# Attention's output products as column tiles: two of 64 for the values, four of 32 for the feature sums

## The chip, the cores and the metric

One core of a Trainium2 chip runs the whole program. The metric is the device time in microseconds of one execution; the figure for a kernel is the median of its runs. The engines are TensorE (PE, with its weight loads listed apart as PEld), VectorE (DVE), ScalarE (ACT), GpSimd (POOL) and SyncE (SP), whose queue issues the transfers.

## What is computed

The reference is a linear attention with exponential features, then two multilayer products:

```python
def phi(x):
    proj = np.einsum('bhsd,df->bhsf', x, w_phi)            # 4 x 8 heads, 576 rows, 64 -> 128
    proj = proj - np.max(np.abs(proj), axis=-1, keepdims=True)
    return np.concatenate([np.exp(proj), np.exp(-proj)], axis=-1)
q_p, k_p = phi(q), phi(k)
kv  = np.einsum('bhsf,bhsd->bhfd', k_p, v)
z   = np.sum(k_p, axis=2)
num = np.einsum('bhsf,bhfd->bhsd', q_p, kv)
den = np.einsum('bhsf,bhf->bhs', q_p, z)[..., None] + 1e-06
x   = (num / den)                                           # heads side by side: 2304 x 512
x   = ((x @ w1) * (x @ w2)) @ w3 @ w_out                    # 512 -> 1024 -> 1024 -> 512
x   = np.maximum(x @ w_in, 0) ** 2 @ w2_out                 # 512 -> 2048 -> 512
```

The weights come as float64 and are decoded on the chip.

## The kernel before

**Attention** goes over 16 pairs of heads (4 batches x 4 pairs), one pair a slot. The order of every instruction in a slot is written by hand in the list SLOT (L36): each name is a step, taken for the pair of the slot or, by an offset in the table `steps` (L575), for the pair before or after. So slot t projects the queries and keys of pair t, prepares those of pair t + 1, and makes the output of pair t - 1. All five engines run strictly in that order (manual schedule, L649).

The steps around the change: `project_q` and `project_k0`, `project_k1` are the feature projections. `max_q` (L386), `max_rows` (a transposition on PE, L394) and `max_parts` (L396) make the maxima of the query rows, which go through a transfer to `mrow` and are subtracted on PE in `minus_q`. `keep_values` (L445) copies kv of a pair to SBUF for the products: for each sign and head a 128 x 128 stationary tile whose 128 columns are the 64 values and the feature sum z repeated 64 times. `out00` to `out11` (L452) multiply it with the features of one head and one half (288) of the rows, for both signs; 64 of the output's partitions are the numerators and the other 64 all hold the denominator. `keep00` to `keep11` (L460) copy the banks to SBUF, `denominators` (L465) take one copy of the denominators out by a transposing reduction, `reciprocals` (L475) invert and spread them, `quotients` (L484) multiply on POOL, `store_x` (L498) writes x for two pairs to HBM.

PSUM in attention is a pool "t" of three banks, a pool "o" of two for the products, and three banks of projected queries.

**Weights** are decoded beside all this. One tile of 128 x 512 takes a transfer to one of four `raw` places (L99), one ACT step, four on DVE (L108 to L118) and one on POOL (L123); those that are split into a high and a low part take one more on ACT and POOL. The list `beside` (L542) is decoded in attention by the steps w-1, w0 and w1 of the slots, one tile after another; the list `need` (L528) is fetched by `prefetch` and decoded after it, `many` (L811) tiles in a step (one unless the table says otherwise), as `begin` (L692) finds room among LEFT and RIGHT places.

**After attention** the w3 tiles are transposed and multiplied with w_out (`Fold`, L767), a fold a step in the first eight steps, while the products with w1 and w2 and the folded weight run over five blocks of rows, twice. Then the last two products run over the same blocks (L958).

Of the kernel before, what the change touches and what calls it, by code (L numbers as in the profile page):

```python
# [18 lines left out]
C = 4  # L19
TAIL = 64  # L20
LEFT = 20
RIGHT = 13

# [8 lines left out]
tail_values/0  # L34
""".split()
SLOT = """  # L36
load_kq product_b project_k0 keep_values turn_w3b split_w3b x_load project_q project_k1 less_max_k0 max_q turn_k out00 max_rows x_split0 max_parts w-1 store_x less_max_k1 x_split2 out01 exp_k0 x_split1 keep00 w1 high_k out10 keep01 turn_q0 out11 w1 keep_q0 project_k2 denominators0 keep10 w0 keep11 low_k less_max_k2 values0 gate turn_w3 exp_k1 denominators1 x_split3 exp_k2 w0 w0 w0 turn_q1 reciprocals keep_q1 minus_q product_a0 exp_q0 values1 exp_q1 turn_tails keep_tails split_q split_w3 low_tail low_q product_a1 quotients keep_a load_v tail_values
""".split()


# [1 line left out]
def attention_then_mlps(ctx: ExitStack, tc: tile.TileContext, q, k, v, w_phi, w1, w2, w3, wo, wi2, wo2, out):  # L42
# [31 lines left out]
    def temps(name):  # L74

        turn[0] += 1
        y_of, t_of = pools[turn[0] % 2 % len(pools)], 0
        if len(pools) > 1:
            t_of = 0 if room_t[0] else 1
            assert room_t[t_of], name  # L80
            room_t[t_of] -= 1
            home_t[name] = t_of
        y = y_of.tile([P, 512], I32, tag="dy", bufs=2, name=f"dy_{name}")
        t = pools[t_of].tile([P, 512], I32, tag="dt", bufs=2 if t_of else 3, name=f"dt_{name}")
        return y, t

    def done_t(name):
        room_t[home_t.pop(name, 0)] += 1

    turn, room_t, home_t = [0], [3, 2], {}  # L90


    def decoding(src, name, got):
# [42 lines left out]
    def finish(steps):  # L136
        for _ in steps:
            pass
# [59 lines left out]
    with ExitStack() as actx:  # L198
# [3 lines left out]
        def bank(name, tag="t", bufs=3):  # L202
            return ps.tile([P, 512], F32, tag=tag, bufs=bufs, name=name)
# [186 lines left out]

        def max_rows(z):

            z["pm"] = bank(f"pm_{z['nm']}")[:, 0:P]
            nc.tensor.transpose(z["pm"], z["m1"], ident)  # L394

        def max_parts(z):  # L396
            pm = z["pm"][0:2 * nb]
            m = att.tile([2 * nb, 32], F32, tag="m", name=f"m_{z['nm']}")
            nc.vector.tensor_reduce(m, pm.rearrange("p (a r) -> p r a", a=4), AX.X, ALU.max)
            mh = att.tile([2 * nb, 2, 32], F32R, tag="mh", name=f"mh_{z['nm']}")  # L400
            nc.vector.tensor_copy(mh[:, 0], m)
            nc.vector.tensor_tensor(out=mh[:, 1], in0=m, in1=mh[:, 0].bitcast(F32), op=ALU.subtract)
            z["mrow"] = mrow
            for s in range(2):
                nc.sync.dma_start(
                    z["mrow"][s:s + 1].bitcast(F32).rearrange("s (k r) -> s k r", r=32), mh[:, s].bitcast(F32)
                )
# [36 lines left out]

        def keep_values(z):  # L445

            z["kv"] = att.tile([P, 2, 2, P], F32, tag="kv", name=f"kv_{z['nm']}")
            kv = z["kv"].rearrange("p s j (h d) -> p s (j h) d", d=D)
            nc.scalar.copy(kv[:, :, 0::3, :], z["pkv"][:, :, :, 0:D])
            nc.scalar.copy(kv[:, :, 1:3, :], z["pkv"][:, :, :, D:].to_broadcast([P, 2, 2, D]))  # L450

        def out_half(z, j, s):  # L452
            z["po", j, s] = po = bank(f"po_{z['nm']}_{j}_{s}", "o", 2)
            for e in range(2):
                nc.tensor.matmul(  # L455
                    po[:, 0:HALF], z["kv"][:, e, j, :], z["qp"][:, e, j, s * HALF:(s + 1) * HALF],
                    start=e == 0, stop=e == 1,
                )

        def keep_half(z, j, s):  # L460
            if j + s == 0:
                z["nd"] = att.tile([P, 2, S], F32, tag="nd", name=f"nd_{z['nm']}")
            nc.scalar.copy(z["nd"][:, j, s * HALF:(s + 1) * HALF], z["po", j, s][:, 0:HALF])

        def denominators(z, j):  # L465

            if j == 0:
                z["dc"] = att.tile([P, nb], F32, tag="dc", name=f"dc_{z['nm']}")
            nc.vector.tensor_reduce(
                z["dc"][j * D:(j + 1) * D],  # L470
                z["nd"][(1 - j) * D:(2 - j) * D, j].rearrange("p (n r) -> p n r", r=32),
                AX.X, ALU.max, apply_transpose=True,
            )

        def reciprocals(z):  # L475
            rc = att.tile([P, nb], F32, tag="rc", name=f"rc_{z['nm']}")
            nc.vector.tensor_scalar(out=rc, in0=z["dc"], scalar1=1e-6, scalar2=None, op0=ALU.add)
            nc.vector.reciprocal(rc, rc)
            z["rb"] = att.tile([P, S], F32, tag="rb", bufs=1, name=f"rb_{z['nm']}")
            nc.vector.transpose(  # L480
                z["rb"].rearrange("p (n r) -> p n r", r=32), rc.unsqueeze(2).to_broadcast([P, nb, 32])
            )

        def quotients(z):  # L484
            b, pr = z["b"], z["pr"]
            if pr % 2 == 0:
                xm[b] = unit(F32, [2, C * P], f"xm_{b}_{pr // 2}")
            for j in range(2):
                h = slice(j * D, (j + 1) * D)
                nc.gpsimd.tensor_tensor(  # L490
                    out=xm[b][h, pr % 2, :], in0=z["nd"][h, j, 0:C * P], in1=z["rb"][h, 0:C * P], op=ALU.mult
                )
                nc.gpsimd.tensor_tensor(
                    out=xt[h, pr, b * TAIL:(b + 1) * TAIL], in0=z["nd"][h, j, C * P:], in1=z["rb"][h, C * P:],
                    op=ALU.mult,
                )

        def store_x(z):  # L498
            b, pr = z["b"], z["pr"]
# [5 lines left out]
        def w3_of(i):  # L505
            kc, g = divmod(i, 2)
            return w3[kc * P:(kc + 1) * P, g * 512:(g + 1) * 512], f"w3_{i}"
# [17 lines left out]
                return got, decode_splitting(src, name, w12, lambda *a: take(*a)), 1  # L525
            return got, decode_splitting(w2_of(i), f"w2_{i}", got, lambda *a: take(*a)), 1

        need = [("w3", 2), ("w3", 3), ("w12", 6), ("w3", 4), ("w3", 5), ("w12", 7)]  # L528
        need += [("w3", i) for i in range(6, 2 * NG)] + [("w12", i) for i in range(8, 2 * NG)]
        need += [("w2", i) for i in range(2 * NR)]  # L530
        reserve, owed, room_raw = [5], [0], [4]
# [1 line left out]
        def prefetch(n=4):  # L533
            while need and room_raw[0] and len(loaded) < n:
                room_raw[0] -= 1
                kind, i = need.pop(0)
                got, steps, places = plan(kind, i)
                next(steps)
                loaded.append((kind, i, got, steps, places))
# [1 line left out]

        beside = [decode_splitting(rows(wo, j), f"wo{j}", wos) for j in range(NG)]  # L542
        beside += [decode_splitting(*w12_of(i), w12) for i in range(6)]
        beside += [decoding(*w3_of(i), w3s) for i in range(2)]
        beside.append(iter(()))
        load_kq(0)
        minus = att.tile([P, P], F32R, bufs=1, name="minus")
        nc.vector.memset(minus.bitcast(F32), -1.0)
# [22 lines left out]
        def even(f, *at):  # L571
# [7 lines left out]
            "turn_k": (1, turn_k), "high_k": (1, high_k), "low_k": (1, low_k),  # L579
            "split_q": (2, split_q), "low_q": (2, low_q), "low_q0": (2, lambda z: low_q(z, nc.vector)),  # L580
            "turn_tails": (1, turn_tails), "keep_tails": (1, keep_tails), "low_tail": (1, low_tail),
            "tail_values": (0, tail_values), "reciprocals": (-1, reciprocals), "quotients": (-1, quotients), "store_x": (-2, store_x),
            "load_kq": (2, lambda z: load_kq(live.index(z))), "load_v": (2, load_v),
        }
        for j in range(2):
            steps[f"turn_q{j}"] = 1, lambda z, j=j: turn_q(z, j)
            steps[f"keep_q{j}"] = 1, lambda z, j=j: keep_q(z, j)
            steps[f"values{j}"] = 0, lambda z, j=j: values(z, j)
            steps[f"denominators{j}"] = -1, lambda z, j=j: denominators(z, j)
            for s in range(2):  # L590
                steps[f"out{j}{s}"] = -1, lambda z, j=j, s=s: out_half(z, j, s)
                steps[f"keep{j}{s}"] = -1, lambda z, j=j, s=s: keep_half(z, j, s)
        for j in range(3):
            steps[f"project_k{j}"] = 0, (even if j == 2 else lambda f, j: lambda z: f(z, j))(project_k, j)
            steps[f"less_max_k{j}"] = 0, (even if j == 2 else lambda f, j: lambda z: f(z, j))(less_max_k, j)
# [53 lines left out]
        with tc.manual_schedule(engines=mine):  # L649
            for entry in START:  # L650
                name, t = entry.split("/")
                step(name, int(t))
            for t in range(len(todo) + 2):
                for name in SLOT:
                    if f"{name}/{t}" not in START:
                        step(name, t)
                if t >= len(todo) - 1:
                    prefetch(t - len(todo) + 3)
        finish(beside[-1])


    late = ctx.enter_context(tc.tile_pool(name="late", bufs=2, side="right", reuse_waits="tile"))
# [29 lines left out]
    def begin(n):  # L692

        fresh, room = [], free["u"] + free["w"] - reserve[0] - owed[0]
        while loaded and len(fresh) < n and loaded[0][4] <= room:
            room -= loaded[0][4]
            owed[0] += loaded[0][4]
            fresh.append(loaded.pop(0))
        return fresh
# [108 lines left out]
    HG = NG // 2  # L808
    steps = [(grp, at, k) for grp in range(2) for at in range(len(order)) for k in range(HG)]
    folds = {i: i for i in range(NG)}  # L810
    many = {10: 0, 11: 0, 30: 0, 31: 0, 40: 0, 0: 3, 1: 3, 2: 2, 3: 2, 4: 2, 5: 2, 6: 2, 37: 2, 38: 2, 39: 2}  # L811
    mlp2 = mains + [tail]

    def evict_first(b, n, yp):
# [223 lines left out]
```

## Time and profile before

| | us |
|---|---|
| median of 3 runs | 983.41 |
| lowest, highest | 981.69, 985.55 |
| the profiled execution | 982.8 |
| its span on the core | 981.0 |

The profile is of one execution. Busy time counts instructions; a matmul's end is modelled, so that neighbours overlap in the list, and the pace of a run of matmuls is read from their starts or from the chain of waits. An idle engine is put down to whoever released it last.

### The profile page before, as it was taken

What the parts mean: (1) busy time and instruction counts of PE and PEld (TensorE: products, weight loads), DVE (VectorE), ACT (ScalarE), POOL (GpSimd) and SP (SyncE); (2) the same over time, 40 slices, a digit from 0 to 9 for tenths busy, and PEclk for the clock granted to TensorE, in tenths of its full rate; (3) what the DMA queues carried; (4) which work ended last, traced back from release to release, by engine and by line L of the source; (5) the groups of instructions that cost most, each with busy time, mean ns of one, the idle gap of its engine ahead of it and who ended that gap; (6) DMA issues with size and microseconds to landing.
All of it is one profiled execution on the core that took longest, in us unless ns stands there. A gap on an engine that the chain in (4) does not pass through costs nothing.

```text
span 981.0 us, 13030 instructions
## 1 busy us (share of the span) xinstructions
PE 961.5 (98%) x4944; PEld 813.3 (83%) x4944; DVE 571.6 (58%) x910; ACT 409.6 (42%) x785; POOL 252.6 (26%) x238
## 2 busy tenths in 40 slices
PE   7999999998999999999999999999999999999997
PEld 6999999986888898888888878888888888888896
DVE  6899999879756456657766488742224222322332
ACT  6888888863422343333333334432223222322322
POOL 3455555534221223333423145510000000000000
PEclk9999999999999999999999999999999999999999
DMA  6344444425232142452444432202001000100010
GB/s 177 107 132 138 130 143 133 147 87 173 85 129 65 66 163 94 150 194 81 134 165 162 165 131 87 86 1 86 0 1 55 32 1 1 64 1 1 8 37 22
DMA packets 68560, 89.11 MB, mean 91 GB/s; under 512 B 27985, under 2 KB 53137, under 8 KB 68497
## 3 DMA queue, kind: packets, MB, share of 16 engines
q1 hardware_dynamic: 68496, 88.28, 28.1%
q8 instruction: 39, 0.64, 0.3%
q14 instruction: 25, 0.20, 0.1%
HBM read 69.76 MB, written 18.35 MB: 90 GB/s over the span
## 4 chain that ended last, share of the span: by engine, by line
PE 93%; DVE 4%; issue 1%; POOL 0%; DMA 0%; ACT 0%; DVEq 0%; POOLq 0%
PE op L858 21%; PE ph L177 20%; PE pa L177 10%; PE pb L177 10%; PE yp L840 9%; PE po L455 6%; PE pkv L431 5%; PE pf L797 4%; PE pk L238 2%; PE pq L379 2%; PE pqt L310 1%; DVE dt_w L111 1%; PE pq L412 1%; PE pw L171 1%; PE pkt L293 1%
## 5 line engine op out<-in xcount | busy, mean ns | idle before, releaser
L858 PE MATMUL op<-w_w,r 128*128 128x512 f32 x864 | 215.1, 396 | 2.3 <-DVE yp L826 2.2
L858 PEld LDWEIGHTS op<-w_w,r 128*128 128x128 f32 x864 | 162.1, 189 | 39.7 <-ACT w_w L131 2.6
L982 DVE SCALAR_TENSOR_TENSOR r<-ph,t 128x512 f32<-128x512 f32 (+1 forms) x80 | 51.0, 638 | 200.4 <-ACT t L980 200.4
L177 PE MATMUL ph<-y,w_w 128*128 128x512 f32 (+1 forms) x768 | 166.0, 365 | 0.0
L177 PEld LDWEIGHTS ph<-y,w_w 128*128 128x128 f32 x768 | 133.3, 188 | 26.1
L980 ACT ACTIVATE t<-ph 128x512 f32<-128x512 f32 (+1 forms) x80 | 44.4, 555 | 223.9 <-PE ph L177 223.9
L840 PE MATMUL yp<-g,w3o 128*128 128x512 f32 (+1 forms) x480 | 108.4, 375 | 0.0
L840 PEld LDWEIGHTS yp<-g,w3o 128*128 128x128 f32 x480 | 84.5, 190 | 16.3
L123 POOL TENSOR_TENSOR dt_w<-dt_w,dy_w 128x512 f32<-128x512 f32 x48 | 63.0, 1312 | 130.9 <-DVE dy_w L118 117.6
L177 PE MATMUL pa<-c,w_w12a 128*128 128x512 f32 (+1 forms) x432 | 95.3, 369 | 0.0
L177 PE MATMUL pb<-c,w_w12b 128*128 128x512 f32 (+1 forms) x432 | 93.9, 366 | 0.0
L177 PEld LDWEIGHTS pa<-c,w_w12a 128*128 128x128 f32 x432 | 75.0, 188 | 15.3 <-ACT c L142 0.4
L177 PEld LDWEIGHTS pb<-c,w_w12b 128*128 128x128 f32 x432 | 75.2, 189 | 13.4
L990 DVE TENSOR_TENSOR r<-r,r 128x512 fp32r<-128x512 f32 (+1 forms) x80 | 51.0, 637 | 42.6 <-ACT r L988 37.9
L919 DVE TENSOR_TENSOR g<-pb,a 128x512 f32<-128x512 f32 (+1 forms) x39 | 24.8, 635 | 84.0 <-PE pb L177 83.8
L988 ACT ACTIVATE r<-r 128x512 fp32r<-128x512 f32 (+1 forms) x80 | 47.2, 590 | 59.6 <-DVE r L982 59.6
L133 POOL TENSOR_TENSOR w_w<-dt_w,w_w 128x512 fp32r<-128x512 f32 x32 | 48.5, 1517 | 90.7 <-ACT w_w L131 90.7
L455 PE MATMUL po<-qp,kv 128*128 128x288 f32 x256 | 68.8, 406 | 0.0
L431 PEld LDWEIGHTS pkv<-vs,kp 128*128 128x128 f32 x512 | 61.3, 192 | 1.0 <-DVE kp L362 0.2
L921 ACT ACTIVATE g<-g 128x512 fp32r<-128x512 f32 (+1 forms) x39 | 23.0, 589 | 91.3 <-DVE g L919 91.3
L431 PE MATMUL pkv<-vs,kp 128*128 128x65 f32 x512 | 60.6, 271 | 0.0
L911 ACT COPY a<-pa 128x512 f32<-128x512 f32 (+1 forms) x39 | 21.2, 543 | 81.3 <-PE pa L177 81.3
(132 smaller groups left out, 1405.7 us busy)
## 6 DMA issues: line engine op xcount, KB each, us to landing
x<-x_hbm SPq DMA_DIRECT2D x16, 512.0 KB
raw_w<-in_moe_w_dram SPq DMA_DIRECT2D x16, 512.0 KB
raw_w<-in_moe_w_in_dram SPq DMA_DIRECT2D x16, 512.0 KB
raw_w<-in_moe_w_out_dram SPq DMA_DIRECT2D x16, 512.0 KB
qm<-in_q_dram SPq DMA_DIRECT2D x16, 256.0 KB
km<-in_k_dram SPq DMA_DIRECT2D x16, 256.0 KB
vs<-in_v_dram SPq DMA_DIRECT2D x32, 128.0 KB
raw_wo<-in_moe_w_out_dram SPq DMA_DIRECT2D x8, 512.0 KB
```

The lines of the kernel that those rows point to most:

```text
L123: nc.gpsimd.tensor_tensor(out=w, in0=t.bitcast(F32), in1=e.bitcast(F32), op=ALU.add)
L133: nc.gpsimd.tensor_tensor(out=dst[:, 1], in0=w[0], in1=dst[:, 0].bitcast(F32), op=ALU.subtract)
L177: nc.tensor.matmul(ps[:, 0:n], a, c, start=kk + i == 0, stop=kk == KD - 1 and i == 2)
L431: nc.tensor.matmul(z["pkv"][:, s, j], z["kp", j][:, c, s, :], z["vs"][:, j, c, :], start=j + s + c == 0, stop=False, skip_group_check=True,)
L455: nc.tensor.matmul(po[:, 0:HALF], z["kv"][:, e, j, :], z["qp"][:, e, j, s * HALF:(s + 1) * HALF], start=e == 0, stop=e == 1,)
L797: nc.tensor.matmul(pf, a, c, start=g + j + n == 0, stop=g == 1 and j == 3 and n == 2)
L840: nc.tensor.matmul(blk.yp[i][:, 0:blk.n], a, d, start=c % HG + s == 0, stop=c % HG == HG - 1 and s == 2)
L858: nc.tensor.matmul(ops[i], a, d, start=j + s == 0, stop=j == NR - 1 and s == 2)
L980: nc.scalar.activation(t[:, 0:n], ph[:, 0:n], AF.Relu)
L982: nc.vector.scalar_tensor_tensor(out=r32[:, 0:n], in0=ph[:, 0:n], scalar=0.0, in1=t[:, 0:n], op0=ALU.max, op1=ALU.mult)
L988: nc.scalar.activation(r[:, 0, 0:n], r32[:, 0:n], AF.Copy)
L990: nc.vector.tensor_tensor(out=r[:, 1, 0:n], in0=r32[:, 0:n], in1=r[:, 0, 0:n].bitcast(F32), op=ALU.subtract)
```

## The change

For each pair the stationary tiles of 128 columns are replaced by tiles of 64 columns (values) and of 32 columns (the feature sum, repeated 32 times). The value products of the two heads write partitions 0 to 63 and 64 to 127 of one bank; one bank for each half of the rows. The four feature sums (two heads, two halves) write four groups of 32 partitions of one more bank, which DVE reads directly. The reciprocals, nine columns wide, are copied to the partitions of their heads by eight small POOL copies (`spread`). The quotients then need two instructions on full partitions instead of four.

With it come a new order of the slot, the transposed maxima in pool "o", a second reduction in `max_parts` instead of a cast, two more w3 tiles in the list `beside` and two fewer in `need`, a prefetch count lower by one in the last slots, one weight place less (RIGHT), two more temporary tiles (dt) on that side, a bound on the tiles begun by the free temporaries, and one tile decoded instead of two in step 39.

```diff
-RIGHT = 13
+RIGHT = 12
 SLOT = """
-load_kq product_b project_k0 keep_values turn_w3b split_w3b x_load project_q project_k1 less_max_k0 max_q turn_k out00 max_rows x_split0 max_parts w-1 store_x less_max_k1 x_split2 out01 exp_k0 x_split1 keep00 w1 high_k out10 keep01 turn_q0 out11 w1 keep_q0 project_k2 denominators0 keep10 w0 keep11 low_k less_max_k2 values0 gate turn_w3 exp_k1 denominators1 x_split3 exp_k2 w0 w0 w0 turn_q1 reciprocals keep_q1 minus_q product_a0 exp_q0 values1 exp_q1 turn_tails keep_tails split_q split_w3 low_tail low_q product_a1 quotients keep_a load_v tail_values
+load_kq product_b project_q keep_values project_k0 turn_w3b split_w3b x_load max_q project_k1 turn_k less_max_k0
+max_rows x_split0 max_parts w-1 store_x high_k out0 less_max_k1 x_split2 exp_k0 out1 x_split1 keep0 feature_sums w1
+keep1 turn_q0 w1 low_k keep_q0 project_k2 w0 less_max_k2 values0 gate turn_w3 exp_k1 denominators x_split3 exp_k2
+spread w0 w0 w0 turn_q1 keep_q1 turn_tails keep_tails minus_q product_a0 exp_q0 reciprocals values1 exp_q1 split_q
+split_w3 low_tail low_q product_a1 quotients keep_a load_v tail_values
 """.split()
...
-        t = pools[t_of].tile([P, 512], I32, tag="dt", bufs=2 if t_of else 3, name=f"dt_{name}")
+        t = pools[t_of].tile([P, 512], I32, tag="dt", bufs=4 if t_of else 3, name=f"dt_{name}")
...
-    turn, room_t, home_t = [0], [3, 2], {}
+    turn, room_t, home_t = [0], [1, 4], {}
...
-            z["pm"] = bank(f"pm_{z['nm']}")[:, 0:P]
+            z["pm"] = bank(f"pm_{z['nm']}", "o", 2)[:, 0:P]
...
-            nc.vector.tensor_copy(mh[:, 0], m)
+            nc.vector.tensor_reduce(mh[:, 0], pm.rearrange("p (a r) -> p r a", a=4), AX.X, ALU.max)
...
+            z["kv"] = att.tile([P, 2, 2, D], F32, tag="kv", name=f"kv_{z['nm']}")
+            nc.scalar.copy(z["kv"], z["pkv"][:, :, :, 0:D])
+            z["zs"] = att.tile([P, 2, 2, 32], F32, tag="zs", name=f"zs_{z['nm']}")
+            nc.scalar.copy(z["zs"], z["pkv"][:, :, :, D:].to_broadcast([P, 2, 2, 32]))
+
+        def out_half(z, s):
+            z["po", s] = po = bank(f"po_{z['nm']}_{s}", "o", 2)
             for e in range(2):
+                for j in range(2):
+                    nc.tensor.matmul(
+                        po[j * D:(j + 1) * D, 0:HALF], z["kv"][:, e, j, :],
+                        z["qp"][:, e, j, s * HALF:(s + 1) * HALF], start=e == 0, stop=e == 1,
+                    )
+
+        def feature_sums(z):
+            z["pd"] = pd = bank(f"pd_{z['nm']}", "o", 2)
+            for e in range(2):
+                for i in range(4):
+                    j, s = divmod(i, 2)
+                    nc.tensor.matmul(
+                        pd[i * 32:(i + 1) * 32, 0:HALF], z["zs"][:, e, j, :],
+                        z["qp"][:, e, j, s * HALF:(s + 1) * HALF], start=e == 0, stop=e == 1,
+                    )
+
+        def keep_half(z, s):
+            nc.scalar.copy(z["nd"][:, s * HALF:(s + 1) * HALF], z["po", s][:, 0:HALF])
+
+        def denominators(z):
+            dc = att.tile([P, nb // 2], F32, tag="dc", name=f"dc_{z['nm']}")
             nc.vector.tensor_reduce(
+                dc, z["pd"][:, 0:HALF].rearrange("p (n r) -> p n r", r=32), AX.X, ALU.max, apply_transpose=True
+            )
+            nc.vector.tensor_scalar(out=dc, in0=dc, scalar1=1e-6, scalar2=None, op0=ALU.add)
+            z["rc"] = att.tile([P, nb // 2], F32, tag="rc", name=f"rc_{z['nm']}")
+            nc.vector.reciprocal(z["rc"], dc)
+
+        def spread(z):
+            z["rc2"] = att.tile([P, 2, nb // 2], F32, tag="rc2", name=f"rc2_{z['nm']}")
+            for i in range(4):
+                for s in range(2):
+                    at = 2 * (i // 2) + s
+                    nc.gpsimd.tensor_copy(
+                        z["rc2"][i * 32:(i + 1) * 32, s, :], z["rc"][at * 32:(at + 1) * 32, :]
+                    )
...
-            for j in range(2):
-                h = slice(j * D, (j + 1) * D)
+            nc.gpsimd.tensor_tensor(
+                out=xm[b][:, pr % 2, :], in0=z["nd"][:, 0:C * P], in1=z["rb"][:, 0:C * P], op=ALU.mult
+            )
+            nc.gpsimd.tensor_tensor(
+                out=xt[:, pr, b * TAIL:(b + 1) * TAIL], in0=z["nd"][:, C * P:], in1=z["rb"][:, C * P:], op=ALU.mult
+            )
...
-        need = [("w3", 2), ("w3", 3), ("w12", 6), ("w3", 4), ("w3", 5), ("w12", 7)]
+        need = [("w12", 6), ("w3", 4), ("w3", 5), ("w12", 7)]
...
-        beside += [decoding(*w3_of(i), w3s) for i in range(2)]
-        beside.append(iter(()))
+        beside += [decoding(*w3_of(i), w3s) for i in range(4)]
...
-                    prefetch(t - len(todo) + 3)
+                    prefetch(t - len(todo) + 2)
...
         fresh, room = [], free["u"] + free["w"] - reserve[0] - owed[0]
+        n = min(n, sum(room_t))
...
-    many = {10: 0, 11: 0, 30: 0, 31: 0, 40: 0, 0: 3, 1: 3, 2: 2, 3: 2, 4: 2, 5: 2, 6: 2, 37: 2, 38: 2, 39: 2}
+    many = {10: 0, 11: 0, 30: 0, 31: 0, 40: 0, 0: 3, 1: 3, 2: 2, 3: 2, 4: 2, 5: 2, 6: 2, 37: 2, 38: 2, 39: 1}
```

## Rows read from the trace of the kernel before

**Rows 1.** The page: busy time and instructions; PE's 40 slices in tenths.
```profile
PE 961.5 (98%) x4944; PEld 813.3 (83%) x4944; DVE 571.6 (58%) x910; ACT 409.6 (42%) x785; POOL 252.6 (26%) x238
...
PE   7999999998999999999999999999999999999997
```

**Rows 2.** Windows: stretch, its length, busy us (instructions) by engine, PEclk, DMA, GB/s.
```profile
100.00:150.00 50.00, 50.00 (x356) 46.29 (x356) 45.37 (x79) 40.80 (x86) 28.32 (x33) 1.00 0.46 133
...
200.00:225.00 25.00, 24.93 (x133) 20.81 (x132) 17.91 (x30) 13.79 (x26) 8.30 (x11) 1.00 0.27 85
...
225.00:250.00 25.00, 20.22 (x87) 16.42 (x86) 21.29 (x29) 7.40 (x13) 11.79 (x10) 0.93 0.62 205
```

**Rows 3.** Chain of waits, 0 to 260 us: start, us, what.
```profile
109.30 0.72 PE pk L238 x6
...
110.01 1.04 PE pq L379 x6
...
112.21 0.97 PE po L455 x4
...
122.00 0.70 PE pk L238 x6
...
215.50 3.90 PE po L455 x16
...
236.60 3.75 PE yp L840 x12
...
252.32 2.77 PE yp L840 x12
```

**Rows 4.** Groups of instructions by line, of the whole span.
```profile
L455 PE MATMUL po<-qp,kv 128*128 128x288 f32 x256 | 68.8, 406 | 0.0
...
L490 POOL TENSOR_TENSOR xm<-nd,rb 64x512 f32<-64x512 f32 x32 | 40.8, 1276 | 10.0 <-DVE rb L480 8.9
...
L463 ACT COPY nd<-po 128x288 f32<-128x288 f32 x64 | 25.5, 398 | 10.1 <-PE po L455 7.4 <-POOL xt L493 2.0 <-PE pm L394 0.8
...
L469 DVE TRANSPOSE_TENSOR_REDUCE dc<-nd 64x18 f32<-64x576 f32 x32 | 24.7, 773 | 2.5 <-ACT nd L463 1.6
...
L493 POOL TENSOR_TENSOR xt<-nd,rb 64x64 f32<-64x64 f32 x32 | 11.5, 359 | 0.0
...
L399 DVE TENSOR_REDUCE m<-pm 36x32 f32<-36x128 f32 x16 | 4.5, 281 | 8.1 <-PE pm L394 8.1
```

**Rows 5.** Timeline of one slot: start, us, engine, line, operation.
```profile
110.05 0.69 DVE L355 TENSOR_REDUCE kmax<-pk 128x4 f32<-128x512 f32 x1 [0.16 <-PE pk L238]
...
110.78 0.69 DVE L362 TENSOR_TENSOR kp<-pk,kmax 128x512 f32<-128x512 f32 x1
...
111.38 1.37 DVE L386 TRANSPOSE_TENSOR_REDUCE m<-pq 128x36 f32<-128x1152 f32 x1
...
111.50 1.29 ACT L368 ACTIVATE kp<-kp 128x512 f32<-128x512 f32 x2 [0.89 <-DVE kp L362]
```

**Rows 6.** Waits of PE: us in total, times, longest.
```profile
PE pw L171 <- POOL dt_w12a L123: 4.8, 1, 4.8
...
PE op L858 <- DVE yp L826: 2.2, 1, 2.2
```

**Rows 7.** Timeline of the passage behind attention; idle time before and its releaser in brackets.
```profile
226.91 0.33 SPq L501 DMA_DIRECT2D x_hbm<-xm  x1
...
232.44 0.69 ACT L106 ACTIVATE dy_w<-raw_w 128x512 f32<-128x512 f32 x1 [10.43 <-DMA raw_w<-in_moe_w_dram]
...
234.30 0.59 ACT L142 ACTIVATE w3o<-pf 128x512 fp32r<-128x512 f32 x1
```

**Rows 8.** Timeline where the last products begin.
```profile
572.87 0.41 DVE L108 TENSOR_SCALAR dt_w<-dy_w 128x512 int32<-128x512 int32 x1
...
575.48 0.69 DVE L118 SCALAR_TENSOR_TENSOR dy_w<-raw_w,dy_w 128x512 f32<-128x512 uint32 x1
...
578.91 4.58 PE L858 MATMUL op<-w_w,r 128*128 128x512 f32 x12 [2.23 <-DVE yp L826]
```

More of the change, by code (lines that the diff above doesn't have):

```diff
@@ L445, in keep_values @@
         def keep_values(z):
[L447 to L453, printed above, removed]
-            for e in range(2):
[L455 to L468, printed above, removed]
+            z["kv"] = att.tile([P, 2, 2, D], F32, tag="kv", name=f"kv_{z['nm']}")
+            nc.scalar.copy(z["kv"], z["pkv"][:, :, :, 0:D])
@@ new lines, in feature_sums @@
+        def feature_sums(z):
[8 more added lines that the diff above has]
+        def keep_half(z, s):
+            if s == 0:
+                z["nd"] = att.tile([P, S], F32, tag="nd", name=f"nd_{z['nm']}")
+            nc.scalar.copy(z["nd"][:, s * HALF:(s + 1) * HALF], z["po", s][:, 0:HALF])
@@ L469, in denominators @@
+        def denominators(z):
+            dc = att.tile([P, nb // 2], F32, tag="dc", name=f"dc_{z['nm']}")
             nc.vector.tensor_reduce(
-                z["dc"][j * D:(j + 1) * D],
-                z["nd"][(1 - j) * D:(2 - j) * D, j].rearrange("p (n r) -> p n r", r=32),
-                AX.X, ALU.max, apply_transpose=True,
-            )
+                dc, z["pd"][:, 0:HALF].rearrange("p (n r) -> p n r", r=32), AX.X, ALU.max, apply_transpose=True
+            )
+            nc.vector.tensor_scalar(out=dc, in0=dc, scalar1=1e-6, scalar2=None, op0=ALU.add)
+            z["rc"] = att.tile([P, nb // 2], F32, tag="rc", name=f"rc_{z['nm']}")
+            nc.vector.reciprocal(z["rc"], dc)
@@ L475, in reciprocals @@
+        def spread(z):
[6 more added lines that the diff above has]
+                    )
         def reciprocals(z):
-            rc = att.tile([P, nb], F32, tag="rc", name=f"rc_{z['nm']}")
-            nc.vector.tensor_scalar(out=rc, in0=z["dc"], scalar1=1e-6, scalar2=None, op0=ALU.add)
@@ L478, in reciprocals @@
-            nc.vector.reciprocal(rc, rc)
             z["rb"] = att.tile([P, S], F32, tag="rb", bufs=1, name=f"rb_{z['nm']}")
             nc.vector.transpose(
-                z["rb"].rearrange("p (n r) -> p n r", r=32), rc.unsqueeze(2).to_broadcast([P, nb, 32])
+                z["rb"].rearrange("p (n r) -> p n r", r=32),
+                z["rc2"].rearrange("p s n -> p (s n)").unsqueeze(2).to_broadcast([P, nb, 32]),
             )
@@ L487, in quotients @@
                 xm[b] = unit(F32, [2, C * P], f"xm_{b}_{pr // 2}")
-            for j in range(2):
-                h = slice(j * D, (j + 1) * D)
[L490 to L496, printed above, removed]
+            nc.gpsimd.tensor_tensor(
[4 more added lines that the diff above has]
+            )
         def store_x(z):
@@ L581, in attention_then_mlps @@
             "turn_tails": (1, turn_tails), "keep_tails": (1, keep_tails), "low_tail": (1, low_tail),
-            "tail_values": (0, tail_values), "reciprocals": (-1, reciprocals), "quotients": (-1, quotients), "store_x": (-2, store_x),
+            "tail_values": (0, tail_values), "reciprocals": (-1, reciprocals),
+            "feature_sums": (-1, feature_sums), "denominators": (-1, denominators), "spread": (-1, spread), "quotients": (-1, quotients), "store_x": (-2, store_x),
             "load_kq": (2, lambda z: load_kq(live.index(z))), "load_v": (2, load_v),
@@ L588, in attention_then_mlps @@
             steps[f"values{j}"] = 0, lambda z, j=j: values(z, j)
[L589 to L592, printed above, removed]
+            steps[f"out{j}"] = -1, lambda z, j=j: out_half(z, j)
+            steps[f"keep{j}"] = -1, lambda z, j=j: keep_half(z, j)
         for j in range(3):
@@ L657, in attention_then_mlps @@
                 if t >= len(todo) - 1:
-                    prefetch(t - len(todo) + 3)
-        finish(beside[-1])
+                    prefetch(t - len(todo) + 2)
+        for steps_ in beside[-2:]:
+            finish(steps_)
     late = ctx.enter_context(tc.tile_pool(name="late", bufs=2, side="right", reuse_waits="tile"))
```

## Prediction

> **What bounds the kernel now.** Read the page first: TensorE (PE) is busy for 98% of the span, and its row of slices is 9 all along except at the two ends and for one 8 at the passage from attention to the products behind it [rows 1]. The windows say what that share is made of [rows 2]: from 100 to 150 us PE is busy for all 50.00, VectorE (DVE) for 45.37 and ScalarE (ACT) for 40.80; from 225 to 250 PE loses 4.8 us, and its mean granted clock of 0.93 means a seventh of that stretch at the lower level, 1.2 GHz, after PE had stood idle. So in attention PE sets the pace with two engines close behind, and what leaves PE's stream there leaves the time, as long as nobody else becomes late.
>
> The chain of waits gives the pace itself [rows 3]. Two slots in a row begin their key projection at 109.30 and at 122.00, so a slot with the extra half projection takes 12.70 us. The output products stand in it as plain sums of matmuls: four records in 0.97 us. The run of 16 at 215.50 takes 3.90, so one record costs 0.244 us, whatever the 0.406 us in the grouped lines says [rows 4]: that longer figure has the way through the array in it, and 0.406 - 0.244 = 0.16 us of each is hidden by the next. There are 256 records for 128 matmuls of the code (16 pairs, two heads, two halves, two signs): each fp32 matmul is two records, one after the other. The products cost 16 x 0.244 = 3.90 us of each slot, 62 us in all.
>
> **The tiles.** Column counts are cut (128 to 64 and 32) and instruction counts doubled: 8 matmuls (16 records) for the two heads, 8 more (16 records) for the sums. A record streams the same 288 columns, so I price it at the same 0.244 us. No row of this trace shows a tile narrower than 128 columns, so whether neighbours run at once is bounded from both sides. All at once: 16/2 + 16/4 = 12 record times, 2.93 us, a gain of 0.97 per slot. Not at all: 32 record times, 7.81 us, a loss of 3.90 per slot. I take the first as likeliest: the two tiles write different partitions and alternate in the order of issue, so nothing in their data ties one to the other.
>
> A change of tile shape may also empty the array. The nearest price is the hidden 0.16 us, from nothing to 0.16 for each of three changes per slot (128 to 64, 64 to 32, back). I take one as seen (0.16): the other two fall into the waits of the next paragraph or overlap with them. The Trainium skill (TensorEngine Tiling (Array Packing), Key Properties) says that changing the tiling mode drains TensorE; by that rule all three would count, 0.49 us a slot and 7.8 us over 16 pairs, and the sum would end 5.3 us higher; no row here shows such a change.
>
> **What waits in the new order.** The transposed row maxima move into the pool of two banks that the products use, so the banks go round: maxima, first half, second half, sums. The second half needs the bank that max_parts reads on DVE; the sums need the bank that keep0 empties on ACT. Put a slot's zero at project_q. PE: the same four pieces that now fill 109.30 to 112.21 (project_q 1.04, two key projections of 0.72, and 0.43 left for the four transpositions of turn_k) take 2.91, and one transposition more, 0.11, is max_rows; the first half starts at 3.0 and is through at 4.0 [rows 3]. DVE: the maximum of 1.37 starts at about 1.2, after the last projection matmul's way through the array, then 0.69 and 0.69 of less_max_k0, then two reductions of 0.28 each: 4.5 [rows 4, 5]. So the second half would wait 0.5. ACT: exp_k0 can start at 3.95 and takes 1.29, keep0 0.40: 5.64, so the sums wait some 0.16 more. Together up to 0.68 us, below that nothing if DVE and ACT run ahead of these sums; I take the middle, 0.34. Behind the waiting second half on PE's queue stand the sums, turn_q0 and the values, so all of it is on the path.
>
> Attention: (0.97 - 0.34 - 0.16) x 16 = 7.5 us gained. Bounds: 15.5 gained (no wait, no emptying) to 0 (0.97 - 0.68 - 0.32 is about 0).
>
> **What costs nothing.** DVE loses one of two 0.77 us reductions per pair and the other is half as long; from 1,152 columns in 1.37 and 576 in 0.77 a column costs about 1.04 ns, so 288 take some 0.47 (an estimate from those two): DVE goes from 0.91 of a slot to about 0.83. ACT loses two evictions of 0.40 and half a copy. GpSimd (POOL) loses one 1.28 and one 0.36 us quotient per pair and gains eight copies of 32 x 9 elements; the nearest row is 0.36 (64 columns), so the eight take from nothing to 2.9 us, and I take 1.6, since a copy of nine columns has little but fixed cost: a balance of zero [rows 4]. These are hidden by PE, which is busy for every microsecond of the slot; if PE fell to DVE's pace the cover would be gone, but DVE's some 10.5 us of 12.7 leave 2 us. The new wait is reciprocals on POOL's copies: behind it on DVE stand low_tail and the next max_q. The copies are issued ahead of three decode steps, of which DVE has over 2 us to do, so it is met in time.
>
> **The passage to the multilayer products.** PE waits 4.8 us for the second w3 pair [rows 6], and the 12 matmuls after it take 3.75 against 2.77 at full clock [rows 3]: 5.8 us in all. With the two tiles decoded in the last two slots their DVE work (some 2.5 us each) goes to a stretch where DVE is busy for 17.91 of 25 [rows 2], and the transposes could start at once. What is late next is the eviction of the first folded weight: ACT copies it at 234.30, behind a decode step that sat 10.43 us for its DMA until 232.44, whose load SyncE could only issue behind the store of x at 226.91 [rows 7]. Store, loads and that place in ACT's queue stay; two loads of raw tiles move to earlier slots, but the prefetch count is one lower in each, so another pair stands in the same place. The wait would end near 235 again. I take 1.5 gained, between 0 and 5.8.
>
> **The second passage.** PE waits 2.2 us for the add that empties the last accumulators, and the 12 matmuls behind it take 4.58 where 2.77 is usual [rows 3, 6, 8]. On DVE a second tile's decoding runs from 572.87 to 576.17, 3.3 us, just ahead of that add. With one tile for that step instead of two it comes later, the add moves up by more than 2.2, and both losses can go: 2.2 + 1.8 = 4.0 at most; I take 3.5. One weight place less delays decodings elsewhere; PE hides them as long as a tile is there when its step begins, and the row for a miss is again 2.2 to 4.0.
>
> **Sum.** The profiled execution took 982.8 (span 981.0 and 1.8 around it), 0.6 under the median. 982.8 - 7.5 - 1.5 - 3.5 = 970.3, so 970; this case alone reaches from 958 (15.5, 5.8 and 4.0 gained) to 978.
>
> **Rivals.** First, only half overlap. An fp32 matmul is two records on one tile [rows 4]. If records start only in program order, the second record of a tile must wait for the first, and the next tile waits behind it: then the second of one runs beside the first of the next, and n matmuls take n + 1 record times. The products take 9 and the sums 9, 18 x 0.244 = 4.39 against 3.90. That is 0.49 lost per slot without waits; with the bank wait of 0.27 that remains between the halves (4.5 less 4.25), one time more for the separated halves and 0.16 for emptying it is 1.16. Over 16 pairs 7.8 to 18.6, less the 5.0 of the passages: 986 to 996. For it: the two records of an fp32 matmul always stand side by side in the trace, and no record starts out of order. Against it: every row is of full-width matmuls, which share one tile and had no choice. It decides once two neighbours share less than half of their time. The Trainium skill (TensorE: Matmul & The Clock Gate, Part 3, What overlaps and what doesn't) says that matmuls start and end in program order and that tiles overlap all the same; the one speaks for this rival, the other against the next, and no row here has two tiles.
>
> Second, the waits eat the gain: full overlap, but the whole 0.68 and two emptyings. Attention gives 0, the passages 0 to 5: 978 to 983. For it: the bank order above, and DVE at 0.91. Against: the same sums assume that each engine starts a slot with nothing done.
>
> Third, no overlap: 3.90 x 16 = 62 lost, 5 gained, 1040. Nothing in the trace excludes it.
>
> **How the numbers follow.** Overlap with part of the waits 0.53; the waits eat it 0.16; half overlap 0.24; none 0.07. Half a per cent, 4.9 us, is about what a measurement of this kernel can tell. Faster (under 978.5): all of the first and 0.05 of the second, 0.58. Within: 0.11 of the second and 0.05 of half overlap, 0.16. Slower: the rest, 0.26. The range reaches from 958 to 992, which leaves out none overlapping, the worse part of half overlap and a little below.
>
> **What would show it.** The products' records under two or four tile widths with starts in pairs, 8 records in about 1 us; if a half takes 1.2 and the sums 2.2, half overlap is right. PE's list of waits: the second half for DVE's m, the sums for ACT's nd; a slot near 12.2 instead of 12.7. At the first passage PE waiting for ACT's w3o instead of a POOL tile; at the second no wait for yp. The prediction is wrong if a slot is 12.7 or longer, or if PE waits for DVE's reciprocals or a weight tile that came late.

## The result

| | median us | lowest, highest |
|---|---|---|
| before (8 runs of this comparison) | 984.31 | 981.69, 987.26 |
| after (8 runs) | 990.19 | 989.36, 994.41 |

The ratio is 1.0071, with an interval of 1.0047 to 1.0095: slower, where 970 was forecast. The profiled execution took 994.36 (span 992.4), 4.2 over its median. Some 3 of these are at its start, where PE waited 1.7 us for the first maxima and then ran at the lower level (granted clock 0.50, 1.2 GHz) from 20 to 25 us: its second projection of queries begins at 23.96, and in the profile of run 6 below, with the same order, at 20.88. This is left out of what follows.

The page of the changed kernel, its engines and its chain's shares by engine, beside [rows 1]:

```profile
PE 962.6 (97%) x5200; PEld 793.6 (80%) x5200; DVE 540.4 (54%) x894; ACT 397.4 (40%) x753; POOL 271.4 (27%) x334
...
PE 83%; ACT 8%; DVE 5%; issue 2%; DMA 1%; POOL 0%; SPq 0%; ACTq 0%; DVEq 0%; POOLq 0%
```

A window of the changed kernel beside [rows 2], columns as there:

```profile
100.00:150.00 50.00, 48.07 (x403) 38.82 (x402) 35.52 (x69) 35.85 (x75) 33.21 (x55) 1.00 0.46 130
```

PE is no longer busy for all of a slot (48.07 of 50), no other engine has taken its place (DVE 35.52, ACT 35.85, both less than before), and ACT holds 8% of the chain, where before it had next to nothing:

```profile
PE 93%; DVE 4%; issue 1%; POOL 0%; DMA 0%; ACT 0%; DVEq 0%; POOLq 0%
```

That is the picture of a ring: engines that wait for each other in turn. The chain, beside [rows 3], shows one turn of it, its pace and the price of the first passage:

```profile
115.82 1.32 PE pq L383 x6
...
117.17 1.38 DVE m L390
118.55 0.59 DVE kmax L359
...
120.38 1.19 PE po L461 x8
121.58 1.12 PE pd L472 x16
122.69 0.60 PE pqt L314 x4
...
123.32 0.60 ACT qT L322
...
127.06 2.05 ACT qp L424 x2
...
129.15 1.35 PE pq L383 x6
...
141.92 1.33 PE pq L383 x6
...
249.61 5.07 PE yp L862 x12
```

The turn goes from the projection of queries (`pq`) over DVE's maxima of the queries and of the keys (`m`, `kmax`) and the reading of the transposed maxima to the second half of the products (`po`), the sums (`pd`) and turn_q0 (`pqt`) on PE; behind turn_q0 ACT works from keep_q0 (`qT`) to the queries' exponentials (`qp`); and behind these stands the next projection of queries. A slot with the extra half projection now takes 13.33 us from one projection of queries to the next (12.70 before), the next one 12.77 (12.47, by this row of the chain before and [rows 3]):

```profile
134.47 0.72 PE pk L238 x6
```

The list of PE's waits beside [rows 6]:

```profile
PE pw L175 <- ACT a L933: 7.7, 1, 7.7
...
PE po L461 <- DVE mh L405: 3.4, 15, 0.9
PE pq L383 <- ACT qp L424: 3.4, 7, 0.5
...
PE op L880 <- ACT r L1010: 0.3, 1, 0.3
```

The second passage has lost its wait (0.3 for 2.2), the first has a longer one (7.7 for 4.8), and two new ones stand in the slots.

The slot itself, from its timeline:

```profile
115.81 0.99 PEld L383 LDWEIGHTS pq<-qT,wss 128*128 128x128 f32 x6 [0.32 <-ACT qp L424]
...
117.17 1.38 DVE L390 TRANSPOSE_TENSOR_REDUCE m<-pq 128x36 f32<-128x1152 f32 x1 [2.03 <-PE pq L383]
...
119.01 1.19 PE L461 MATMUL po<-qp,kv 128*64 128x288 f32 x8
...
119.88 1.29 ACT L372 ACTIVATE kp<-kp 128x512 f32<-128x512 f32 x2 [0.28 <-DVE kp L366]
...
120.38 1.19 PE L461 MATMUL po<-qp,kv 128*64 128x288 f32 x8 [0.18 <-DVE mh L405]
...
121.52 1.18 PE L472 MATMUL pd<-qp,zs 128*32 128x288 f32 x16
...
122.62 0.66 PE L314 MATMUL pqt<-ident,qs 128*128 128x128 f32 x4
```

The products run from 119.01 to 122.62, 3.61 us with their waits, where the full-width ones took 3.90. The tiles do overlap, and fully: 16 records for the sums are through in 1.10 us. A narrower window shows four of them starting within 0.05 us of each other (0.45 less the 0.41 that one such record takes in the list):

```profile
121.52 0.45 PE L472 MATMUL pd<-qp,zs 128*32 128x288 f32 x4
```

So the loss is not in the tiles. At the slot's head DVE has stood idle for 2.03 us, until the projection of queries gives it something to do; that projection has itself waited for exp_q1 on ACT (its weight load, `PEld`, for 0.32); and exp_k0 starts on ACT 4.06 us after the slot's head.

### The profile page after: what moved, and what is told of

Same layout as the page of the kernel before. It is cut to its first block, busy times and chain, and to the rows that moved or that the text cites. A ratio compares the mean times of both kernels' runs of the same rounds, so it can differ in the third digit from the quotient of the medians.

```text
span 992.4 us, 13580 instructions
## 1 busy us (share of the span) xinstructions
PE 962.6 (97%) x5200; PEld 793.6 (80%) x5200; DVE 540.4 (54%) x894; ACT 397.4 (40%) x753; POOL 271.4 (27%) x334
## 4 chain that ended last, share of the span: by engine, by line
PE 83%; ACT 8%; DVE 5%; issue 2%; DMA 1%; POOL 0%; SPq 0%; ACTq 0%; DVEq 0%; POOLq 0%
PE ph L181 20%; PE op L880 20%; PE yp L862 10%; PE pa L181 10%; PE pb L181 10%; PE pf L819 4%; ACT qp L424 3%; DVE m L390 2%; PE pq L383 2%; ACT kp L372 2%; PE po L461 2%; PE pd L472 2%; ACT qT L322 1%; PE pqt L314 1%; DVE kmax L359 1%
## 5 line engine op out<-in xcount | busy, mean ns | idle before, releaser
L498 POOL COPY rc<-rc 32x9 f32<-32x9 f32 x128 | 44.2, 345 | 36.7 <-DVE rc L490 32.1
```

The lines of the kernel that those rows point to most:

```text
L498: nc.gpsimd.tensor_copy(z["rc2"][i * 32:(i + 1) * 32, s, :], z["rc"][at * 32:(at + 1) * 32, :])
```

## The experiments

The theory after this reading: the new order, with the projection of queries first, loses the time (**order**). Its rival is the prediction's own doubt: the changes of tile shape and the wait of the second half for its bank eat the gain and more (**tiles**).

**1. The tiles alone, in the old order.** Decoding and pool of the maxima as before:

```diff
-... project_q project_k1 less_max_k0 max_q turn_k out00 max_rows ... out01 exp_k0 ... keep00 w1 high_k out10 keep01 turn_q0 out11 ...
+... project_q project_k1 less_max_k0 max_q turn_k out0 max_rows ... out1 exp_k0 ... keep0 w1 high_k feature_sums keep1 turn_q0 ...
```

> The column tiles alone, in the order of the kernel before (key projection first, maxima in the pool of three banks), decoding as before. If the order is what lost the time (the queries' projection at the head of a slot waits for exp_q1, which still reads the three banks), the slots fall to 12.2 to 12.45 us and the time to 978 to 982. If the changes of tile shape are what lost it, the slots stay at 12.9 or more and the time at 988 or more.

Measured: 977.2 us, ratio 0.9920 (0.9891 to 0.9950), a little under the first range. PE's timeline in one slot:

```profile
109.41 0.60 PE L293 MATMUL pkt<-ident,km 128*128 128x128 f32 x4
109.93 1.19 PE L457 MATMUL po<-qp,kv 128*64 128x288 f32 x8
111.06 0.33 PE L394 MATMUL pm<-ident,m 128*128 128x128 f32 x1
111.31 1.19 PE L457 MATMUL po<-qp,kv 128*64 128x288 f32 x8
112.44 1.18 PE L468 MATMUL pd<-qp,zs 128*32 128x288 f32 x16
113.54 0.66 PE L310 MATMUL pqt<-ident,qs 128*128 128x128 f32 x4
```

Nothing waits in this slot. Each half takes 1.13 us to the next start and the sums 1.10, where four record times are 0.97. What is over (0.16, 0.16, 0.13, and 0.14 and 0.08 in front of the halves) stands at each of five changes of tile shape. The Trainium skill (TensorEngine Tiling (Array Packing), Key Properties) says that a change of tiling mode drains TensorE; these rows agree, at 0.08 to 0.16 us a change. By the sums of the slot the tiles save 3.90 - 3.36 - 0.22 = 0.32 us. From one slot to the next the chain gives less:

```profile
107.11 0.70 PE pk L238 x6
...
119.55 0.71 PE pk L238 x6
...
131.76 0.70 PE pk L238 x6
...
229.68 2.81 PE yp L857 x12
```

The slots take 12.44 and 12.21 us where they took 12.70 and 12.47, so 0.26 is saved in each, 4.2 us over 16 pairs. The measured 6.3 us hold more than that: at the first passage PE's wait is 3.1 us for 4.8, and the 12 matmuls behind it take 2.81 for 3.75 [rows 3]. So only about two thirds of what this run gains is gained in attention.

**2. The new head of the slot alone,** on the full-width products:

```diff
-load_kq product_b project_k0 keep_values ... project_q project_k1 less_max_k0 max_q turn_k out00 max_rows
+load_kq product_b project_q keep_values project_k0 ... max_q project_k1 turn_k less_max_k0 out00 max_rows
```

> The kernel before with its full-width products; only the queries' projection and max_q move ahead of the key projection, as in the new order. If the order is the cause: PE waits for exp_q in most slots, slots of 12.9 to 13.1, 989 to 992. If the tiles are the cause: slots of 12.6 and 983 to 986.

Measured: 998.2, ratio 1.0135 (1.0101 to 1.0170). More than foreseen, and not in the way foreseen: no wait for exp_q stands in PE's list, and the longest new one is for an eviction.

```profile
119.50 1.29 ACT L368 ACTIVATE kp<-kp 128x512 f32<-128x512 f32 x2 [2.61 <-DVE kp L362]
...
121.14 1.24 PE L455 MATMUL po<-qp,kv 128*128 128x288 f32 x4 [0.25 <-ACT nd L463]
```

ACT has been idle for 2.61 us before exp_k0, because less_max_k0 now stands behind max_q on DVE; the eviction keep00 stands behind exp_k0, and PE waits for its bank.

**3, 4. Each half of that swap alone,** to part PE's order from DVE's:

```diff
 # PE's: the queries' projection first, DVE as before
-project_k0 keep_values ... project_q project_k1 less_max_k0 max_q
+project_q keep_values project_k0 ... project_k1 less_max_k0 max_q
 # DVE's: max_q first, PE as before
-project_q project_k1 less_max_k0 max_q turn_k out00
+project_q max_q project_k1 turn_k less_max_k0 out00
```

> The kernel before with one swap on PE: the queries' projection ahead of the key projection, DVE's order as it was (less_max_k0 ahead of max_q). If the head of PE's slot is what costs (PE waits there for exp_q1, DVE waits for its first data), most of the 15 us of both swaps together: 992 to 998. If DVE's order is what costs, 983 to 987.

> The kernel before with the other swap alone: max_q (1.37 us) ahead of less_max_k0 on DVE, PE's order as it was. If DVE's order is what costs (exp_k0 on ACT starts 1.4 us or more later, the evictions keep00 and keep01 stand behind it, and PE waits for their banks): 992 to 998, PE's longest wait that of the products for ACT's nd. If the head of PE's slot is: 983 to 987.

Measured: 1002.2, ratio 1.0198 (1.0175 to 1.0222), and 1005.8, ratio 1.0232 (1.0212 to 1.0252). Both expectations of an innocent half were wrong: each half alone costs more than both together. PE's waits with PE's order changed:

```profile
PE pm L394 <- DVE m L386: 12.6, 16, 1.2
```

And with DVE's order changed:

```profile
PE pm L394 <- DVE kp L362: 10.3, 14, 0.7
PE po L455 <- ACT nd L463: 5.6, 15, 2.1
```

With PE's order alone, less_max_k0 must wait for the later key projection and max_q behind it is late for max_rows (12.6 us in 16 times). With DVE's alone, the keys must wait behind max_q, and the maxima wait for the bank that the keys hold (10.3), the products for the late eviction (5.6). The old order projects the keys first and lets DVE work on them while PE projects the queries. Each of the three orders tried here that give this up makes either the keys' exponentials or the maxima late.

**5. The maxima back in the pool of three banks,** in the changed kernel:

```diff
-            z["pm"] = bank(f"pm_{z['nm']}", "o", 2)[:, 0:P]
+            z["pm"] = bank(f"pm_{z['nm']}")[:, 0:P]
```

> The changed kernel with the transposed maxima back in the pool of three banks; the queries' projection stays at the head of the slot. If the prediction's bank wait (the second half waits for DVE's reading of the maxima, 0.23 us a slot in the trace) is what lost the time, 986 to 987. If the projection at the head of the slot is, because exp_q1 must end first and all that follows hangs on it, the wait only moves: 989 to 993.

Measured: 1002.7, ratio 1.0194 (1.0170 to 1.0217): neither. The move of the maxima, which the prediction counted as a wait, saves some 12 us in this order:

```profile
PE pm L398 <- DVE kp L366: 13.7, 14, 1.0
```

In the old pool max_rows gets the bank of the first key projection, and must wait until DVE has read it, up to 1.0 us, in 14 slots (13.7 in all).

**6. The changed kernel with the old decoding:** RIGHT, `need`, `beside`, the prefetch count, the temporaries and `many` as before.

> The changed kernel with the decoding of the kernel before (two w3 tiles in attention, RIGHT 13, two tiles in step 39). If the moved w3 tiles made the first passage longer, the stretch from the last projection of queries to the first folded product falls from 42.2 to about 38.2 us, and the second passage gives back 3.6: 989 to 991. If the passage is longer because of the order of attention, it stays at 42 and the time rises to 993 to 995.

Measured: 987.9, ratio 1.0045 (1.0017 to 1.0073). PE's wait at the first passage is 2.8 us instead of 7.7; the wait at the second is back (2.2). The time is a little under the first range: the decoding made the first passage longer.

**7. One tile less in step 39 alone,** on the kernel before:

```diff
-    many = {... 38: 2, 39: 2}
+    many = {... 38: 2, 39: 1}
```

> The kernel before with one tile decoded in step 39 instead of two. If that alone ends the wait at the second passage: no wait for yp in PE's list, 3 to 4 us less, 980 to 982. If another wait takes its place: 983 to 985.

Measured: 979.0, ratio 0.9960 (0.9938 to 0.9983), and no wait for yp in PE's list. Of its 4.5 us, 4.0 are the 2.2 of the wait and the 1.8 that PE lost behind it at the lower clock [rows 8]; from 580 to 585 us the kernel before has a mean granted clock of 0.67.

**8. All of the decoding, on the kernel before:**

> The kernel before (full-width products, old order) with all of the decoding changes. If these lose at the first passage what they gain at the second: 985 to 987, PE waiting 7 to 8 us for the second w3 pair and not at all for yp. If the first passage is as short as in the kernel before: 979 to 980.

Measured: 984.3, ratio 1.0015 (1.0001 to 1.0029); PE waits 8.5 us at the first passage. So the decoding changes other than that of step 39 lose about 5.3 us there (984.3 less 979.0), in the old order and with full-width products as well. The moved w3 tiles, the weight place less, the temporaries and the prefetch count were not parted here.

**9, 10. The changed kernel in the old order, and with the old prefetch count as well.** Run 9 takes back the whole order of the slot and, with it, the move of the maxima to pool "o"; run 10 adds this:

```diff
-                    prefetch(t - len(todo) + 2)
+                    prefetch(t - len(todo) + 3)
```

> The changed kernel with all of its decoding, in the order of the kernel before. If order and decoding are two separate losses, 979 to 981 (the 977.2 of the tiles in the old order, and the 2.3 by which the changed kernel is over itself with the old decoding), PE waiting 7 to 8 us for the second w3 pair. If the long first passage was only a result of the new order, 973 to 975.

> The same, with the prefetch count of the last slots as in the kernel before (one more tile in each). If the passage is long because the third tile of the first step is loaded only behind the store of x, and its decode step then stands ahead of the first folded weight on ACT, PE's wait falls from 7 to 8 to 3 to 5 us: 975 to 977. If it is long for want of temporaries or room, nothing changes: 979 to 981.

Measured: 979.0, ratio 0.9953 (0.9936 to 0.9971), and 977.9, ratio 0.9945 (0.9924 to 0.9966). The first is as foreseen, and says that order and decoding are separate losses. The second fell short: PE's wait is 7.0 for 7.8, and the 1.1 us between the two times are within their intervals. ACT's timeline at the passage, in the first of the two:

```profile
225.14 0.67 ACT L106 ACTIVATE dy_w<-raw_w 128x512 f32<-128x512 f32 x1 [5.02 <-POOL dt_w L123]
...
232.25 0.67 ACT L106 ACTIVATE dy_w<-raw_w 128x512 f32<-128x512 f32 x1 [6.44 <-DMA raw_w<-in_moe_w_dram]
...
233.68 0.67 ACT L106 ACTIVATE dy_w12b<-raw_w12b 128x512 f32<-128x512 f32 x1 [0.76 <-DMA raw_w12b<-in_moe_w_dram]
...
236.13 0.67 ACT L106 ACTIVATE dy_w<-raw_w 128x512 f32<-128x512 f32 x1 [1.79 <-DMA raw_w<-in_moe_w_dram]
236.71 0.58 ACT L142 ACTIVATE w3o<-pf 128x512 fp32r<-128x512 f32 x1
```

And in the second:

```profile
221.94 0.68 ACT L106 ACTIVATE dy_w<-raw_w 128x512 f32<-128x512 f32 x1 [0.52 <-DMA raw_w<-in_moe_w_dram]
...
227.46 0.67 ACT L106 ACTIVATE dy_w12b<-raw_w12b 128x512 f32<-128x512 f32 x1 [4.84 <-DMA raw_w12b<-in_moe_w_dram]
...
230.95 0.67 ACT L106 ACTIVATE dy_w<-raw_w 128x512 f32<-128x512 f32 x1 [2.83 <-DMA raw_w<-in_moe_w_dram]
231.53 0.57 ACT L142 ACTIVATE w3o<-pf 128x512 fp32r<-128x512 f32 x1
```

In the second the step that waited 6.44 us for the load behind the store starts at 221.94 after 0.52 us, but other decode steps still stand ahead of the first folded weight (`w3o`) on ACT: one that waits 5.02 us for a temporary which POOL frees, and two that wait 4.84 and 2.83 for their transfers. The kernel before had two steps there that waited for transfers (10.43 [rows 7] and 0.61), the first of these runs has three. Which of these steps, taken away alone, would end the wait was not tried.

**11. The two parts that gain, together:** the tiles in the old order, with one tile in step 39.

> Column tiles in the order of the kernel before, and one tile decoded in step 39. If the two gains (6.3 and 4.5 us against the kernel before) lie in different stretches and add, 972 to 974; if the wait at the second passage returns in another place, 976 to 978.

Measured: 972.1, ratio 0.9890 (0.9868 to 0.9912). The gains add, and this version beats both kernels.

**12. Both halves ahead of the maxima** in that version, for two changes of shape less:

```diff
-turn_k out0 max_rows x_split0 max_parts w-1 store_x less_max_k1 x_split2 out1 exp_k0
+turn_k out0 out1 max_rows x_split0 max_parts w-1 store_x less_max_k1 x_split2 exp_k0
```

> The best version so far (tiles, old order, one tile in step 39) with both halves of the values ahead of max_rows, which takes two changes of tile shape out of each slot. If a change costs 0.15 us and nothing else becomes late: slots 0.25 to 0.3 us shorter, 967 to 969. If the maxima, 1.1 us later, bring their transfer to minus_q too late: PE waits for mrow, 972 or more.

Measured: 987.2, ratio 1.0046 (1.0030 to 1.0063), but not for the reason given. PE's waits:

```profile
PE pk L238 <- DVE kp L362: 6.1, 7, 0.9
PE pkv L431 <- DVE kp L362: 6.1, 7, 0.9
```

And a row of DVE's timeline, the first reduction of max_parts:

```profile
110.62 0.28 DVE L399 TENSOR_REDUCE m<-pm 36x32 f32<-36x128 f32 x1 [1.83 <-PE pm L394]
```

The transfer is in time. DVE, in its order, waits 1.83 us for the later maxima, less_max_k1 stands behind, and PE waits up to 0.9 us in 14 slots for the keys that it makes.

## Why the prediction was wrong

**The sum by parts.** Order, with the pool of the maxima: 990.2 (the changed kernel) less 979.0 (run 9), 11.2 us lost. Tiles: 979.0 less 984.3 (9 and 8), 5.3 gained, or 6.3 by run 1. Decoding: 984.3 less 983.0 (8 and its own runs of before), 1.4 lost. Together 7.2 lost; the ratio of 1.0071 is 7.0. The changed kernel was measured beside other runs of the kernel before than runs 8 and 9; by the ratios, 1.0071 and 0.9953, the order loses 11.6.

**The step that failed** is the one on what waits in the new order. It began "Put a slot's zero at project_q", followed each engine from there to the sums, and added the waits that it found to PE's pieces. As far as it went it was close: exp_k0 starts at 4.06 us (3.95 forecast), the reductions of the maxima end at 4.41 (4.5), and the second half waits 0.18 (0.5 at most). What it never asked is when the next project_q can begin. project_q writes the three banks that exp_q1 of the pair before still reads, and exp_q1 ends a run of work on ACT that starts only behind turn_q0. So the way from project_q to the end of exp_q1 bounds a slot, whatever PE's sum is. In the old order (run 1) it nearly fills the slot:

```profile
107.66 1.21 PE L379 MATMUL pq<-qT,wss 128*128 128x384 f32 x6
...
117.72 2.14 ACT L420 ACTIVATE qp<-pq 128x1152 f32<-128x1152 f32 x2
...
120.10 1.21 PE L379 MATMUL pq<-qT,wss 128*128 128x384 f32 x6
```

It takes 12.20 us (107.66 to 119.86) of a slot of 12.44, and 0.24 is to spare (in the kernel before, 12.07 of 12.69: from 109.85 to the end of exp_q1 at 121.92); PE fills the time up to 120.10 with the key projection that stands ahead of project_q. The new order puts that key projection, 0.72 us, behind project_q and so onto this way, and the wait of the second half with it: turn_q0 starts 6.80 us behind project_q (5.88 in run 1), and the way takes 13.29 (115.82 to 129.11) of 13.33. PE's sum per slot is no larger for it, which is why the prediction saw nothing. It charged the order 0.34 us a slot; the order took about 0.7 (11.2 over 16, and two slots of 13.33 and 12.77 where run 1 has 12.44 and 12.21). That the ring sets the slot is read from the chain, and run 9, which takes back order and pool at once, ends it; which of the moved steps, taken back alone, would be enough in the changed kernel was not tried.

**The tiles** were rightly taken to overlap; the rival of half overlap, whose 986 to 996 holds the result, is wrong as a cause: its sums would take 2.2 us, they take 1.10. So it is luck that the stated range of 958 to 992, which reached that far up for this rival, holds the result. The Trainium skill (TensorE: Matmul & The Clock Gate, Part 3, The mechanism and What overlaps and what doesn't) says that tiles overlap although matmuls keep program order; the overlap is in the rows, and that the two records of an fp32 matmul don't hold the next tile back is what they add. But the gain itself was mis-sized: of the 0.97 us a slot, about 0.67 went to the changes of shape, of which the prediction counted one of three at 0.16 (the order of run 1 has five), and 0.26 was left.

**The bank wait** of the second half was seen well in place and a little large in size: 0.18 in the slot shown, 3.4 us in 15 times, for 0.34. But the move that causes it is worth some 12 us in this order (run 5).

**The first passage** went the other way: 1.5 us gained was forecast, 5.3 lost (984.3 of run 8 less 979.0 of run 7), or 7.0 (979.0 of run 9 less 972.1 of run 11). The prediction named the right queue, ACT's, with its decode steps ahead of `w3o`, and held that another pair would stand in the same place; three steps wait for transfers there and not two (run 9).

**The second passage** was right: 3.5 gained was forecast, 4.5 measured (run 7).

**What was to cost nothing** did, with one number off: the eight POOL copies take 0.345 us each by the page, 2.8 us a pair, near the upper bound of 2.9, where 1.6 was taken. They are not met in time, as was held: DVE waits 1.0 us for them at `rb` (L504) in a slot. But PE doesn't wait for that in run 1. The row of the page:

```profile
L498 POOL COPY rc<-rc 32x9 f32<-32x9 f32 x128 | 44.2, 345 | 36.7 <-DVE rc L490 32.1
```

## What to carry to other kernels

In a kernel whose engines run in written order, price a new order by the time at which each engine's first work of a round is ready, not by PE's sums: here a swap at the head of a slot cost 15 us in the kernel before with not one instruction added (run 2), and the whole new order gave away more than the tiles earned. Where a step writes a place that the end of the round before still reads, follow that way once around: PE was busy all the time in run 1, and only 0.24 us a slot were to spare. When a change bundles a saving and a new order, run the saving in the old order first. A step moved out of a stretch helps only if the queue that ends the wait there gets shorter; count what stands in it.

## What the runs showed that was not expected

- fp32 matmuls, two records each, on four column tiles of 32: 16 records in 1.10 us, against 3.90 for 16 full-width ones; on two tiles of 64, 8 records in 1.13 (both with a change of shape in them).
- A change of tile shape cost 0.08 to 0.16 us, five times a slot in run 1.
- A GpSimd copy of 32 x 9 elements took 0.345 us, nearly as long as the 0.359 of a 64 x 64 product [rows 4].
- Two swaps that cost 19 and 23 us alone cost 15 together.
